# Rearranging the first microseconds of a fused S5 + SwiGLU kernel: fewer warm-up matmuls, a split first tile, and another order of loads

## The chip, the cores and the metric

The kernel runs on one core of a Trainium2 chip. The metric is the device time of one execution in microseconds (us). Before the change it is 183.48 us, the median of three runs (183.38, 183.48 and 184.09).

A core has a matrix engine (TensorE, in the profile PE, with its weight loads as PEld), a vector engine (VectorE, DVE), a scalar engine (ScalarE, ACT), GpSimd (POOL) and a queue engine that issues most DMAs (SyncE, SP). Each engine executes its own list of instructions in order and waits on semaphores for the others.

## The reference

The input x has 2048 rows of 512 values in bf16. Each row is normalised, and the normalised rows go through two branches whose results are added to x:

```python
xn = layernorm(x)                                   # rows of 512, eps 1e-5
# branch A: a diagonal complex state space model with 512 states
Lam_bar = exp(dt * Lam);  B_bar = ((Lam_bar - 1) / Lam)[:, None] * Bmat
h_t = Lam_bar * h_{t-1} + B_bar @ xn_t              # for t in 0..2047
yA  = 2 * real(h @ Cmat.T) + xn * Dskip
# branch B: a gated feed-forward layer of width 1376
yB  = (silu(xn @ w_gate) * (xn @ w_up)) @ w_down
return x + yA + yB
```

## The kernel before, in words

The 2048 rows are cut into 16 tiles of 128 rows and 4 chunks of 4 tiles. The matrix engine needs the normalised rows transposed (features on the partitions); the buffer for that is `xnT`, two chunks deep. For each chunk the matrix engine computes the gate and the up product (11 slices of w_gate and w_up of up to 128 columns, four matmuls of 512 columns each, line 684), the input product of the state space model (line 750), the down product (line 838, with the Dskip term at line 841 for the first two chunks) and the output product of the state space model (line 854). The vector engine does the normalisation, the rotations and the scans; the scalar engine evicts the products from PSUM.

The program is a graph of tasks. `_schedule` lists them for each engine: the lists of the matrix engine and of SP keep the order in which the tasks were added, and those of the other engines come from a list scheduler that uses estimated durations. `_plan` turns dependences into semaphore waits.

The head of the kernel, which the change touches, is the time until the first full-width matmul of the up product. It goes like this:

- SP issues the loads in this order (lines 405 to 416): x tile 0, x tile 1, x tiles 2-3 as one load of 256 KB, the first three gate slices (`ld_wgA`, 384 KB), the next three (`ld_wg0`, 384 KB), the first six up slices (`ld_wu0`, 768 KB), then the other gate and up slices and x tiles 4-7.
- The matrix engine starts with `pe_warm`: ten matmuls of 512 columns on a zeroed tile, whose results nobody reads (line 451). Then come the transposes of the parameter rows (`params_t`, line 460).
- For each of the tiles 0 to 3, `ln_tile` adds bn_stats (line 473), bn_aggr (line 476) and the variance plus eps (`ve`, line 478) on the vector engine, the power -1/2 (`rstd`, line 480) on GpSimd and the normalisation itself (`xn`, line 483) on the vector engine. In the head, the bn_stats of a tile waits for the `ve` of the tile ahead and for the `xn` of two tiles ahead, by real dependences.
- `ffn_gate_quarters` runs six gate slices of the first chunk tile by tile ("quarters" of 128 columns), so that they can start before all four tiles are there. `xt_tile_fine` transposes one tile with four matrix-engine transposes (line 523) and evicts it with one scalar-engine copy of 128x512 (line 529). The order on the matrix engine is: transposes of tiles 0 and 1; 24 gate matmuls of tile 0 (line 712); transposes of tile 2; 24 gate matmuls of tile 1; transposes of tile 3; 24 of tile 2; 24 of tile 3. The up product (line 684, from `ffn_up`) follows.
- Between these, GpSimd and the vector engine compute the parameters (`dt`, line 586; lines 588 and 591), and the scalar engine makes the first tables (`tm`, line 635). The copy of tile 3 stands behind two of these in the scalar engine's list.

Of the kernel before, what the change touches and what calls it, by code (L numbers as in the profile page):

```python
# [10 lines left out]
ALU = alu_op_type.AluOpType  # L11
# [10 lines left out]
    warm=10,  # L22
# [8 lines left out]
class _Task:  # L31
    __slots__ = ("eng", "fn", "deps", "name", "est", "idx", "dma", "sem", "lvl",
                 "waits", "nsig", "vc", "out", "lat", "bl", "start", "fin", "nbytes", "prio", "ninst")
# [5 lines left out]
class _Graph:  # L39
# [5 lines left out]
    def add(self, eng, fn, reads=(), writes=(), name="", est=100.0, dma=False, after=(), out=False, nbytes=0, prio=0.0, ninst=1):  # L45
# [21 lines left out]
        t.deps = deps  # L67
        t.sem = None
# [12 lines left out]
def _schedule(tasks, engines, slack=200.0):  # L81
    succ = defaultdict(list)
    for t in tasks:
        for d in t.deps:
            succ[d].append(t)
# [18 lines left out]
    nun = {t: len(t.deps) for t in tasks}  # L104
# [135 lines left out]
def bass_parallel_sum__ssm_conv_s5__swiglu_ffn__prompt_kernel(  # L240
# [28 lines left out]
    EPS = 1e-5  # L269
# [3 lines left out]
    with es:  # L273
# [135 lines left out]
        dma("ld_x1", x_sb[:, 1:2, :], x_v[:, 1:2, :], [("x", 1)], TILEB)  # L409
        dma("ld_x2", x_sb[:, 2:4, :], x_v[:, 2:4, :], [("x", 2), ("x", 3)], 2 * TILEB)  # L410
        FQ = 3 * 128
        dma("ld_wgA", wg[:, :, 0:FQ], wg_v[:, :, 0:FQ], [("wg", "a")], 512 * FQ * 2)
        dma("ld_wg0", wg[:, :, FQ:FH0], wg_v[:, :, FQ:FH0], [("wg", 0)], 512 * (FH0 - FQ) * 2)
# [55 lines left out]
        ln_prev = [None]  # L469
        ln_xn = {}  # L470

        def ln_tile(a, norm_act):
            g.add("dve", lambda e, a=a: e.bn_stats(out=st[:, a, :], in_=x_sb[:, a, :]),  # L473
                  reads=[("x", a)], writes=[("st", a)], name="bnst%d" % a, est=640,
                  after=(((ln_prev[0],) if (ln_prev[0] is not None and a < 4) else ()) + ((ln_xn[a - 2],) if (a < 4 and (a - 2) in ln_xn) else ())))
            g.add("dve", lambda e, a=a: e.bn_aggr(out=mv[:, a, :], in_=st[:, a, :]),
                  reads=[("st", a)], writes=[("mv", a)], name="bnag%d" % a, est=90)
            ln_prev[0] = g.add("dve", lambda e, a=a: e.tensor_scalar(out=ve[:, a:a + 1], in0=mv[:, a, 1:2], scalar1=EPS, scalar2=None, op0=ALU.add),  # L478
                                reads=[("mv", a)], writes=[("ve", a)], name="ve%d" % a, est=70)
            g.add("pool", lambda e, a=a: e.tensor_tensor(out=rstd[:, a:a + 1], in0=ve[:, a:a + 1], in1=mhalf[:, a:a + 1], op=ALU.pow),  # L480
                  reads=[("ve", a), ("mhalf",)], writes=[("rstd", a)], name="rstd%d" % a, est=400)
# [4 lines left out]
            else:  # L486
# [3 lines left out]
                      reads=[("x", a), ("rstd", a), ("nmr", a)], writes=[("xn", a % NXN)], name="xn%d" % a, est=710)  # L490

# [4 lines left out]
        def xt_chunk(c):  # L496
            a0 = 4 * c
            for pair in range(2):
# [12 lines left out]
                def evac(e, aa=aa, slot=slot):  # L511
# [3 lines left out]
                      writes=[("xnT", c % 2, aa % 4), ("xnT", c % 2, aa % 4 + 1)], name="xTev%d" % aa, est=930)  # L515

        def xt_tile_fine(c, a):
            if True:
                slot = next_tr()

                def tr4(e, a=a, slot=slot):
                    for kt in range(KT):
                        inst = e.transpose(out=ptr[:, slot, kt * 128:(kt + 1) * 128],  # L523
                                           in_=xn_sb[:, a % NXN, kt * 128:(kt + 1) * 128], identity=ident[:])
                    return inst
                g.add("pe", tr4, reads=[("xn", a % NXN), ("ident",)], writes=BK(slot), name="xT%d" % a, est=4 * 64, ninst=4)

                def evac(e, a=a, slot=slot):
                    return e.activation(out=xnT[:, c % 2, a % 4, :, :],  # L529
                                        in_=ptr[:, slot, 0:512].rearrange("p (k t) -> p k t", k=KT), func=AF.Identity)  # L530
                g.add("act", evac, reads=BK(slot), writes=[("xnT", c % 2, a % 4)], name="xTev%d" % a, est=500)

        def xt_chunk_dma(c):
            s0 = (4 * c) % NXN
            dma("xTd%d" % c, xnT[:, c % 2].rearrange("p j k t -> p (j k) t"), xn_sb[:, s0:s0 + 4, :],
                [("xnT", c % 2, j) for j in range(4)], 4 * TILEB, reads=[("xn", s0 + j) for j in range(4)], xpose=True)
# [135 lines left out]
        def wres(nm, i):  # L672
            if nm == "wg" and i < 3:
                return ("wg", "a")
            return (nm, 0 if i < 6 else 1)

        def ffn_mm(c, i, which):
# [9 lines left out]
            g.add("pe", mm, reads=[wres("wg" if which == "g" else "wu", i)] + [("xnT", c % 2, j) for j in range(4)],  # L687
# [12 lines left out]
        def ffn_gate_quarters(c, tiles):  # L700
            xt_tile_fine(c, 4 * c)
            banks = {i: next_bank() for i in tiles}
            for q in range(4):
                for ii, i in enumerate(tiles):
                    if q < 3 and ii == 0:
                        xt_tile_fine(c, 4 * c + q + 1)
# [3 lines left out]
                    def mm(e, bk=bk, i=i, fs=fs, c=c, q=q):  # L710
                        for kt in range(KT):
# [3 lines left out]
                    g.add("pe", mm, reads=[wres("wg", i), ("xnT", c % 2, q)], writes=BK(bk), name="mm_gq%d_%d_%d" % (c, i, q), est=4 * 62, ninst=4)  # L715
# [29 lines left out]
        def ssm_b_unit(c, pt):  # L745
            br, bi = next_bank(), next_bank()
            for ri, bk in ((0, br), (1, bi)):
# [5 lines left out]
                g.add("pe", mm, reads=[("BT", ri, kt) for kt in range(KT)] + [("xnT", c % 2, j) for j in range(4)],  # L753
# [66 lines left out]
        def dc_chunk(c, mid=None, split_last=False):  # L820
# [10 lines left out]
            for (lt, c0, nc_), bk in zip(items, banks):  # L831
# [11 lines left out]
                g.add("pe", mmA, reads=[("hT", hb, i) for i in range(FT)] + [("wd", 0), ("wd", 1)] + ([("xnT", c % 2, lt)] + [("diagD", kt) for kt in range(KT)] if dg else []),  # L843
# [130 lines left out]
```

## Time and profile before

| what | us |
|---|---|
| median of three runs | 183.48 |
| the profiled execution: span from first to last instruction | 181.8 |
| around the span, against the median | 1.7 |
| PE busy | 177.7 (98% of the span) |
| DVE busy | 165.0 (91%) |
| ACT busy | 91.4 (50%) |
| POOL busy | 13.4 (7%) |

The profiled execution has no time of its own beside its span; what lies around the span is taken as the difference to the median, 183.48 - 181.8 = 1.7 us, and counted as constant.

Times inside the profile are given from the start of the span. In the timeline a row has the start, the duration, the engine and the line, the operation, the tiles written and read, and how many instructions were merged; in brackets stands the idle time ahead of it and what ended it. A matrix-engine instruction is shown with its whole latency, so rows overlap: the step from one matmul to the next is shorter than a row's duration. The names out of the matrix engine are `pb` (PSUM banks); `SPq` and `ACTq` are rows in which a queue issues DMAs.

### The profile page before, as it was taken

The numbers are of one execution on the slowest core, as the hardware profiler recorded it, in microseconds if no ns is written. First come the engines' busy times: TensorE is split into PE (matmuls) and PEld (weight loads), VectorE is DVE, ScalarE is ACT, GpSimd is POOL, SyncE is SP. The second block draws the span as 40 slices with busy tenths as digits, with TensorE's granted clock in tenths as the row PEclk, the third lists the DMA queues.
The fourth block names the chain that finished last, engine by engine and source line by source line (L and its number), as shares of the span: only waits on it lengthen the run. The fifth ranks groups of instructions, "written<-read, shape, count | busy, mean of one in ns | idle before, by whom it ended". The sixth has DMA issues, their size and how long they took to land.

```text
span 181.8 us, 2579 instructions
## 1 busy us (share of the span) xinstructions
PE 177.7 (98%) x937; PEld 86.8 (48%) x937; DVE 165.0 (91%) x359; ACT 91.4 (50%) x162; POOL 13.4 (7%) x30
## 2 busy tenths in 40 slices
PE   6999999999999999999999999999999999999994
PEld 2694444444444454444444455444444444444643
DVE  3899878999999998999999999999999999999733
ACT  3299989996899108057666380026677620000000
POOL 5530500000000013000000220000000000000000
DMA  5992666669100000730000000620000000000102
GB/s 146 325 375 61 141 130 108 145 182 346 49 0 4 0 0 0 128 108 0 0 0 0 0 4 0 115 94 22 0 4 2 2 0 0 0 32 29 58 29 87
DMA packets 23388, 12.39 MB, mean 68 GB/s; under 512 B 15088, under 2 KB 23376, under 8 KB 23376
## 3 DMA queue, kind: packets, MB, share of 16 engines
q1 hardware_dynamic: 23344, 12.23, 25.3%
q8 instruction: 7, 0.11, 0.3%
q14 instruction: 5, 0.04, 0.1%
q10 hardware_dynamic: 32, 0.00, 0.0%
HBM read 6.46 MB, written 2.10 MB: 47 GB/s over the span
## 4 chain that ended last, share of the span: by engine, by line
PE 97%; ACT 0%; POOL 0%; DVE 0%; issue 0%; DVEq 0%; POOLq 0%
PE pb L684 39%; PE pb L838 21%; PE pb L854 15%; PE pb L750 15%; PE pb L712 3%; PE pb L451 2%; PE pb L841 1%; PE pb L523 1%; ACT xnT L529 0%; POOL zt L442 0%; DVE osb L865 0%; PE pb L460 0%; POOL mhalf L432 0%; DVEq L234 0%; POOLq L959 0%
## 5 line engine op out<-in xcount | busy, mean ns | idle before, releaser
L684 PE MATMUL pb<-xnT,wu 128*128 128x512 bf16 (+1 forms) x176 | 43.7, 379 | 0.0
L838 PE MATMUL pb<-wd,hT 128*128 128x512 bf16 (+3 forms) x187 | 39.7, 367 | 0.0
L789 DVE TENSOR_TENSOR_SCAN vq<-sm,car,vq 128x512 bf16<-128x512 f32 x32 | 39.5, 1271 | 0.1
L684 PE MATMUL pb<-xnT,wg 128*128 128x512 bf16 (+1 forms) x152 | 38.4, 379 | 0.0
L734 ACT ACTIVATE uf<-pb 128x512 bf16<-128x512 f32 (+1 forms) x44 | 25.4, 603 | 6.8 <-PE pb L684 6.6
L854 PE MATMUL pb<-W,hss 128*128 128x512 bf16 (+1 forms) x136 | 28.3, 366 | 0.0
L750 PE MATMUL pb<-xnT,BT 128*128 128x512 bf16 x128 | 28.1, 379 | 0.0
L684 PEld LDWEIGHTS pb<-xnT,wu 128*128 128x128 bf16 (+1 forms) x176 | 17.6, 100 | 20.1
L838 PEld LDWEIGHTS pb<-wd,hT 128*128 128x128 bf16 (+1 forms) x187 | 18.0, 98 | 18.5
L697 ACT ACTIVATE sg<-pb 128x512 bf16<-128x512 f32 (+1 forms) x38 | 22.5, 597 | 7.5 <-PE pb L684 7.4
L684 PEld LDWEIGHTS pb<-xnT,wg 128*128 128x128 bf16 (+1 forms) x152 | 15.3, 100 | 17.6
L757 ACT ACTIVATE u_sb<-pb 128x512 bf16<-128x512 f32 x16 | 9.6, 600 | 20.5 <-PE pb L750 20.3
L854 PEld LDWEIGHTS pb<-W,hss 128*128 128x128 bf16 x136 | 13.2, 98 | 13.9
L750 PEld LDWEIGHTS pb<-xnT,BT 128*128 128x128 bf16 x128 | 12.5, 98 | 15.1
L736 DVE TENSOR_TENSOR hT<-sg,uf 128x512 bf16<-128x512 bf16 (+1 forms) x44 | 18.1, 416 | 1.2 <-ACT uf L734 0.7
L480 POOL TENSOR_TENSOR rstd<-ve,mhalf 128x1 f32<-128x1 f32 x16 | 9.4, 604 | 90.4 <-DVE ve L478 90.4
L473 DVE BATCH_NORM_STATS2 st<-x_sb 128x6 f32<-128x512 bf16 x16 | 10.4, 685 | 2.9 <-DMA x_sb<-in_A_x_dram 2.8
L780 DVE TENSOR_TENSOR scrA<-u_sb,cosT 128x1024 bf16<-128x1024 bf16 x16 | 10.9, 682 | 0.7 <-ACT u_sb L759 0.7
L489 ACT ACTIVATE xn_sb<-x_sb,nmr,rstd 128x512 bf16<-128x512 bf16 x8 | 5.9, 803 | 10.2 <-POOL rstd L480 8.8
L799 DVE TENSOR_TENSOR scrA<-vq,sin 128x1024 bf16<-128x1024 bf16 x16 | 11.0, 684 | 0.0
L783 DVE TENSOR_TENSOR scrA<-u_sb,sin 128x1024 bf16<-128x1024 bf16 x16 | 10.9, 684 | 0.0
L795 DVE TENSOR_TENSOR scrA<-vq,cosT 128x1024 bf16<-128x1024 bf16 x16 | 10.9, 684 | 0.0
(71 smaller groups left out, 135.8 us busy)
## 6 DMA issues: line engine op xcount, KB each, us to landing
out_dram<-osb SPq DMA_DIRECT2D x15, 128.0 KB, 1.7
x_sb<-in_A_x_dram SPq DMA_DIRECT2D x3, 512.0 KB, 7.6
wd<-in_B_w_down_dram SPq DMA_DIRECT2D x1, 1280.0 KB, 7.0
wg<-in_B_w_gate_dram SPq DMA_DIRECT2D x2, 384.0 KB, 4.6
wu<-in_B_w_up_dram SPq DMA_DIRECT2D x1, 768.0 KB, 7.4
wg<-in_B_w_gate_dram SPq DMA_DIRECT2D x1, 608.0 KB, 8.5
wu<-in_B_w_up_dram SPq DMA_DIRECT2D x1, 608.0 KB, 9.6
x_sb<-in_A_x_dram SPq DMA_DIRECT2D x2, 128.0 KB, 2.2
```

Source lines behind the costliest of these rows:

```text
L684: inst = e.matmul(pbank[0:fs, bk, :].rearrange("p (j t) -> p j t", j=4), lhsT=w[:, kt, i * 128:i * 128 + fs], rhs=xnT[:, c % 2, :, kt, :], ...
L697: g.add("act", lambda e, sl=sl, bk=bk, fs=fs: e.activation(out=sg[0:fs, sl, :], in_=pbank[0:fs, bk, :], func=AF.Silu), reads=BK(bk), write ...
L734: g.add("act", lambda e, ul=ul, bk=bk, fs=fs: e.activation(out=uf[0:fs, ul, :], in_=pbank[0:fs, bk, :], func=AF.Identity), reads=BK(bk), w ...
L736: g.add("dve", lambda e, sl=sl, ul=ul, fs=fs, i=i, hb=hb: e.tensor_tensor(out=hT[0:fs, hb, i, :], in0=sg[0:fs, sl, :], in1=uf[0:fs, ul, :] ...
L750: inst = e.matmul(pbank[:, bk, :].rearrange("p (j t) -> p j t", j=4), lhsT=BT[:, ri, kt, pt * 128:(pt + 1) * 128], rhs=xnT[:, c % 2, :, kt ...
L780: g.add("dve", lambda e, sl=sl, U=U, Cb=Cb: e.tensor_tensor(out=pr2[:, sl, 0], in0=U, in1=Cb, op=ALU.mult), reads=ru + rdt, writes=[("pr", ...
L783: g.add("dve", lambda e, sl=sl, Usw=Usw, S2=S2: e.tensor_tensor(out=pr2[:, sl, 1], in0=Usw, in1=S2, op=ALU.mult), reads=ru + rdt, writes=[ ...
L789: g.add("dve", lambda e, sl=sl, ri=ri, pt=pt, rr=rr, c=c: e.tensor_tensor_scan(out=vq[:, sl, 1, ri, :], data0=rr[:, pt:pt + 1].to_broadcas ...
L795: g.add("dve", lambda e, sl=sl, Q=Q, Cb=Cb: e.tensor_tensor(out=po2[:, sl, 0], in0=Q, in1=Cb, op=ALU.mult), reads=rq + rdt, writes=[("po", ...
L799: g.add("dve", lambda e, sl=sl, Qsw=Qsw, S2sw=S2sw: e.tensor_tensor(out=po2[:, sl, 1], in0=Qsw, in1=S2sw, op=ALU.mult), reads=rq + rdt, wr ...
L838: inst = e.matmul(pbank[:, bk, 0:nc_], lhsT=hT[0:fs, hb, i, lt * 128:(lt + 1) * 128], rhs=wd[0:fs, i, c0:c0 + nc_], start=(i == 0), stop=F ...
L854: inst = e.matmul(pbank[:, bk, 0:nc_], lhsT=hss[:, hb, pt, ri, lt * 128:(lt + 1) * 128], rhs=W12[:, ri, pt, c0:c0 + nc_], start=False, sto ...
```

## The change

Five edits, all in the head:

1. `warm` goes from 10 to 8: two of the zero matmuls are taken out.
2. The six gate slices come as one load of 768 KB (rows of 1536 bytes instead of twice 768), and this load stands ahead of x tiles 2-3 in SP's list.
3. Tile 0 is transposed and evicted in two halves (two transposes and a copy of 128x256 each), in two PSUM banks. The 24 gate matmuls of tile 0 are cut likewise: 12 that contract over the first half, then the transposes of tile 1, then the 12 that contract over the second half.
4. The transposes of tiles 2 and 3 go into the middle of a tile's gate matmuls: after two of the six slices, the four others follow behind the transposes.
5. The order of the normalisation in the vector engine's list is set by order-only edges (`order=`, no semaphore): bn_stats of tile a behind `ve` of tile a-1, bn_aggr of tile a behind `xn` of tile a-1. The planner's estimate for `rstd` goes from 400 to 600 ns, with a priority for the head.

The order that the planner makes of this: on the matrix engine 8 warm-ups, the parameter transposes, the 4 transposes of tile 0, 12 gate matmuls, the 4 of tile 1, 20 gate matmuls, the 4 of tile 2, 24, the 4 of tile 3, 40, and then the up product as before. On the vector engine the head becomes: bn_stats 0, bn_aggr 0, `ve` 0, bn_stats 1, `xn` 0, bn_aggr 1, `ve` 1, `xn` 1, the copy of the parameters (line 463), bn_stats 2, bn_aggr 2, `ve` 2, bn_stats 3, `xn` 2, bn_aggr 3, `ve` 3, four diagD (line 466), the two parameter operations (before: lines 588 and 591), `xn` 3. GpSimd's and SP's lists are otherwise as before; the scalar engine has one copy more, and the copy of tile 3 again stands behind two `tm`.

```diff
-    warm=10,
+    warm=8,
...
         dma("ld_x0", x_sb[:, 0:1, :], x_v[:, 0:1, :], [("x", 0)], TILEB)
         dma("ld_x1", x_sb[:, 1:2, :], x_v[:, 1:2, :], [("x", 1)], TILEB)
+        dma("ld_wg0", wg[:, :, 0:FH0], wg_v[:, :, 0:FH0], [("wg", 0)], 512 * FH0 * 2)
         dma("ld_x2", x_sb[:, 2:4, :], x_v[:, 2:4, :], [("x", 2), ("x", 3)], 2 * TILEB)
-        FQ = 3 * 128
-        dma("ld_wgA", wg[:, :, 0:FQ], wg_v[:, :, 0:FQ], [("wg", "a")], 512 * FQ * 2)
-        dma("ld_wg0", wg[:, :, FQ:FH0], wg_v[:, :, FQ:FH0], [("wg", 0)], 512 * (FH0 - FQ) * 2)
         dma("ld_wu0", wu[:, :, 0:FH0], wu_v[:, :, 0:FH0], [("wu", 0)], 512 * FH0 * 2)
...
         def ln_tile(a, norm_act):
-            g.add("dve", lambda e, a=a: e.bn_stats(out=st[:, a, :], in_=x_sb[:, a, :]),
-                  reads=[("x", a)], writes=[("st", a)], name="bnst%d" % a, est=640,
-                  after=(((ln_prev[0],) if (ln_prev[0] is not None and a < 4) else ()) + ((ln_xn[a - 2],) if (a < 4 and (a - 2) in ln_xn) else ())))
-            g.add("dve", lambda e, a=a: e.bn_aggr(out=mv[:, a, :], in_=st[:, a, :]),
-                  reads=[("st", a)], writes=[("mv", a)], name="bnag%d" % a, est=90)
...
+            head = a < 4
+            ln_bn[a] = g.add("dve", lambda e, a=a: e.bn_stats(out=st[:, a, :], in_=x_sb[:, a, :]),
+                             reads=[("x", a)], writes=[("st", a)], name="bnst%d" % a, est=640,
+                             order=((ln_ve.get(a - 1),) if head else ()))
+            ln_ag[a] = g.add("dve", lambda e, a=a: e.bn_aggr(out=mv[:, a, :], in_=st[:, a, :]),
+                             reads=[("st", a)], writes=[("mv", a)], name="bnag%d" % a, est=90,
+                             order=((ln_xn.get(a - 1),) if head else ()))
...
-                  reads=[("ve", a), ("mhalf",)], writes=[("rstd", a)], name="rstd%d" % a, est=400)
+                  reads=[("ve", a), ("mhalf",)], writes=[("rstd", a)], name="rstd%d" % a, est=600, prio=(3000.0 if head else 0.0))
...
+        def xt_tile_fine(c, a, parts=1):
+            n = KT // parts
+            for h in range(parts):
                 slot = next_tr()
+                k0 = h * n
+
+                def tr(e, a=a, slot=slot, k0=k0):
+                    for kt in range(k0, k0 + n):
+                        inst = e.transpose(out=ptr[:, slot, (kt - k0) * 128:(kt - k0 + 1) * 128],
                                            in_=xn_sb[:, a % NXN, kt * 128:(kt + 1) * 128], identity=ident[:])
                     return inst
+                g.add("pe", tr, reads=[("xn", a % NXN), ("ident",)], writes=BK(slot), name="xT%d_%d" % (a, h), est=n * 64, ninst=n)
+
+                def evac(e, a=a, slot=slot, k0=k0):
+                    return e.activation(out=xnT[:, c % 2, a % 4, k0:k0 + n, :],
+                                        in_=ptr[:, slot, 0:n * 128].rearrange("p (k t) -> p k t", k=n), func=AF.Identity)
+                g.add("act", evac, reads=BK(slot), writes=(XN(c, a % 4) if parts == 1 else [XN(c, a % 4)[h]]), name="xTev%d_%d" % (a, h), est=130 + 90 * n)
...
         def ffn_gate_quarters(c, tiles):
-            xt_tile_fine(c, 4 * c)
+            xt_tile_fine(c, 4 * c, parts=2)
             banks = {i: next_bank() for i in tiles}
...
+            for q in range(4):
+                if q == 0:
+                    quarter(q, tiles, 0, 1)
+                    xt_tile_fine(c, 4 * c + 1)
+                    quarter(q, tiles, 1, 2)
+                else:
+                    quarter(q, tiles[:2], 0, 2)
+                    if q < 3:
+                        xt_tile_fine(c, 4 * c + q + 1)
+                    quarter(q, tiles[2:], 0, 2)
```

`quarter(q, ts, h0, h1)` adds the gate matmuls of tile q for the slices in `ts` over the halves h0 to h1 of the contraction; `XN(c, j)` names the two halves of tile j in `xnT`. Every other reader of `xnT` now waits for both halves.

## The prediction

> **What bounds the kernel now.** I read the chain that ended last first, in order of time (start, length, engine, tile and line):
>
> ```profile
> 1.42 4.45 PE pb L451 x10
> ...
> 6.63 0.61 ACT xnT L529
> ...
> 7.29 1.59 PE pb L712 x24
> ...
> 10.66 2.68 PE pb L712 x48
> 13.34 13.81 PE pb L684 x64
> 27.15 13.81 PE pb L750 x64
> ```
>
> From line 684 on the chain is the matrix engine without a gap, 13.81 / 64 = 0.216 us a matmul; and no other engine stands in the chain between 7.3 and 179 us. So this change is worth exactly what it does to the start of the first up matmul, provided that nothing later comes to wait. In the timeline that start is 13.18 us (the chain gives 13.34, the end of the piece ahead).
>
> Next the timeline of the head, DVE and ACT rows:
>
> ```profile
> 2.84 0.69 DVE L473 BATCH_NORM_STATS2 st<-x_sb 128x6 f32<-128x512 bf16 x1 [2.84 <-DMA x_sb<-in_A_x_dram]
> 3.97 0.69 DVE L473 BATCH_NORM_STATS2 st<-x_sb 128x6 f32<-128x512 bf16 x1
> 5.28 0.69 DVE L473 BATCH_NORM_STATS2 st<-x_sb 128x6 f32<-128x512 bf16 x1
> 8.00 0.41 DVE L483 TENSOR_SCALAR xn_sb<-x_sb,mv,rstd 128x512 bf16<-128x512 bf16 x1 [0.41 <-POOL rstd L480]
> 8.53 0.15 DVE L478 TENSOR_SCALAR ve<-mv 128x1 f32<-128x1 f32 x1
> 9.41 0.41 DVE L483 TENSOR_SCALAR xn_sb<-x_sb,mv,rstd 128x512 bf16<-128x512 bf16 x1
> 9.93 1.34 ACT L635 ACTIVATE scrC<-iot,sm 128x512 f32<-128x512 f32 x2 [0.20 <-DVE sm L588]
> 11.18 0.57 ACT L529 ACTIVATE xnT<-pb 128x512 bf16<-128x512 bf16 x1
> ```
>
> Tile 2's bn_stats starts at 5.28 because the vector engine is busy, not because x tiles 2-3 are late. Tile 3's copy (11.18) comes in time for the matmuls of tile 3. What starts the gate matmuls at 7.29 is tile 0's copy.
>
> Then the loads. Single issues (start) and their time to landing, asked of one issue each, give the landing times: x tile 0 0.79 + 2.0 = 2.8, x tile 1 1.25 + 2.3 = 3.5, tiles 2-3 1.71 + 3.0 = 4.7, first gate slices 2.18 + 3.9 = 6.1, next ones 2.69 + 5.3 = 8.0, six up slices 3.25 + 7.4 = 10.6. The windows view shows the rate (its last column):
>
> ```profile
> 3.00:4.00 1.00, 1.00 (x4) 0.35 (x3) 0.90 (x4) 0.00 (x0) 0.00 (x0) 1.00 0.91 260
> 4.00:5.00 1.00, 1.00 (x4) 0.40 (x3) 0.96 (x3) 0.00 (x0) 0.56 (x1) 1.00 0.98 282
> 5.00:6.00 1.00, 1.00 (x8) 0.20 (x6) 0.94 (x3) 0.00 (x0) 0.55 (x1) 1.00 0.89 257
> 6.00:7.00 1.00, 0.96 (x11) 0.67 (x8) 0.84 (x5) 0.37 (x1) 0.66 (x1) 1.00 1.06 333
> ```
>
> The DMA engines are full (the column before, 0.89 to 1.06) from 2 us on, and the loads land in the order of issue. A load that is moved back pays for the bytes put ahead of it.
>
> **The change, part by part.**
>
> Two warm-ups less: the chain has 4.45 / 10 = 0.445 us each, so the last one ends near 5.0 instead of 5.86. The parameter transposes follow at about 5.0 and take 0.2. They need the last parameter row; nothing shows when it landed except that the transposes ran at 5.79, so the gain here is 0 to 0.85 us, and I take all but a little of it. It is not on the final path (below).
>
> Tile 0: `xn` 0 now stands ahead of bn_aggr 1 and starts near 4.7 instead of 4.80, ends 5.1. Its transposes run near 5.15 instead of 5.99. A copy of 128x256 has no row; it lies between the 0.21 of a 128x4 ACT row and the 0.60 of 128x512, in proportion to the elements 0.40. The first half is copied by about 6.0, the second, which overlaps it, by 6.4.
>
> The joined gate load: the six up slices have the same shape, and took 10.6 - 8.0 = 2.6 us behind the load ahead of them. Behind x tile 1 that gives 3.5 + 2.6 = 6.1; at the 257 to 282 GB/s of that stretch 786 KB would take 2.8 to 3.1, so 6.3 to 6.6. I take 6.3. The gate matmuls can start at 6.35 instead of 7.29, a gain of 0.9 if nothing came after. Bounds 6.1 to 6.8.
>
> x tiles 2-3: 768 KB now go ahead of them where nothing did. Best row: the joined load by its like (2.6) and their own 4.7 - 3.5 = 1.1 after it, so 3.5 + 2.6 + 1.1 = 7.2. Worst: the same 1280 KB, in the present order and in narrower rows, were complete at 8.0. I take 7.4, nearer to the first because the rows are as wide as there. Call this L; the bounds are 7.0 and 8.0.
>
> Now tile 2 is late, and the vector engine stands at its bn_stats with everything of the head behind it. Its steps from rows: bn_stats at L + 0.03; bn_stats 3 comes 3.97 - 2.84 = 1.13 later and takes 0.69; `xn` 2 follows, start L + 1.89, end L + 2.30 (0.41). GpSimd's `rstd` (0.56) fits between, since `dt` ends before 8. The transposes of tile 2 start at L + 2.35. From there the matrix engine has left, in its new order, 8 transposes and 64 gate matmuls, at (10.27 - 8.93) / 24 = 0.056 us each: 72 x 0.056 = 4.03. So the up product starts at L + 6.38 if it never waits again.
>
> It waits a little. `ve` 3 starts at L + 2.41 (bn_aggr and `ve` follow `xn` 2 by 8.53 - 8.00 = 0.53), four diagD, the two parameter operations now ahead of `xn` 3 (0.15 each at most) and `xn` 3 follow: 9.41 - 8.53 = 0.88, plus 0.17, so `xn` 3 ends at L + 3.87, just as the matrix engine gets there. But the copy of tile 3 stands behind the two `tm` of 1.34 (they start when the first parameter operation is done, L + 3.36, and 11.18 - 9.93 = 1.25 later comes the copy): it starts at L + 4.6, ends L + 5.17, and the last 24 matmuls (1.34) end at L + 6.57. With L = 7.4 the up product starts at 13.97 instead of 13.18: 0.8 us later. Wherever L is above 6.6, the change loses one for one with it.
>
> Between tile 1's first matmuls and tile 2's transposes the matrix engine would stand still for about one us; that, not the copy of tile 0, is the new wait. All matmuls and transposes of real data are kept. The vector engine's order costs nothing by itself, since the DMA wait hides it.
>
> Behind the head: the later loads keep their order and total bytes, the next one landing at about 10, where 13.2 is needed. DVE ends the head L + 3.87 - 0.17 - 9.82 = 1.3 late, half a us more than PE. It has 10 - 7.42 = 2.6 us of idle time between 20 and 30, and waits for ACT's u_sb, which follows PE, at 29.95, so this is absorbed. The nearest deadline later is the DMA transpose of chunk 2 (issued at 71.70 when ACT has normalised, 4.5 to landing, 76.2; PE wants it at 77.11): 0.9 of slack, moving along with both.
>
> Sum: -0.9 (earlier start of the gates) and +1.7 (waits for tiles 2 and 3) = +0.8. The profiled execution's 181.8 and the 1.7 around it make the median, 183.48; prediction 184.3.
>
> **The rivals.**
>
> The pair is early (ends on the other side). If the DMA engines brought x tiles 2-3 before 6.6, the change would do what it says. After x tile 1 (3.5) they must bring 1.05 MB. At the 333 GB/s of the fourth row this takes 3.15 us: L = 6.65 and no change, 183.5. At the 395 GB/s that the windows view shows for 9 to 10 us, L = 6.2 and 183.0. For a gain above 0.5% L would have to be 5.7, 477 GB/s, which no stretch has. Against it: from 3 to 6 us the traffic ran at 257 to 282. [...]
>
> The clock comes late. The warm-ups take 0.445 us each where the up matmuls take 0.216 (half rate), and the transposes at 6.64 still step by about 0.1 us, those at 8.71 by 0.056: full speed came between 6.9 and 7.3. With two warm-ups less and a pause after them it could come later. Ahead of tile 2's transposes stand 36 gate matmuls and transposes: cold they take 3.85 us from 6.35 and end at 10.2, 0.45 past L + 2.35 = 9.75. If the clock is up by then, 184.7; each further us of half rate costs 0.5. For: a longer pause. Against: a like amount of work between 3.5 and 7. [...]
>
> DVE's delay is not absorbed and the transpose of chunk 2 comes late: above 0.9 us of extra delay each us costs one. Up to 185.1. The idle time at 20 to 30 speaks against it.
>
> **How the numbers follow.** Late tile 2: 0.62, 184.3, its own range 183.9 to 184.9 (L from 7.0 to 8.0). Early pair: 0.14, 183.0 to 183.5. Late clock: 0.18, about 184.7. DVE: 0.04; the rest 0.02. I draw the range 183.2 to 185.1. The bound of 0.5%, about what a measurement can tell, is 0.92 us: slower than that needs L above 7.5, some 0.4 of the first case and most of the next, together 0.45. Faster than that: 0.03. Within: 0.52.
>
> **What would show it.** In the profile after: gate matmuls from about 6.3; bn_stats of tile 2 waiting for the DMA at 7.2 to 8.0; a gap of the matrix engine ahead of tile 2's transposes of about one us and a smaller one ahead of the last 24 matmuls, released by ACT; the first up matmul near 14.0; from there the same distances as now. Wrong would be: bn_stats of tile 2 before 6.6, or half-rate steps in the gate matmuls, or a gap of PE after 14.

## The result, and the profile after

The changed kernel takes 185.71 us, the median of five runs (185.54 to 186.44), beside 183.85 us for the kernel before in five runs: ratio 1.012, interval 1.010 to 1.014. The prediction was 184.3 with a range up to 185.1, counted from the 183.48 of the first three runs. From there the loss is 2.2 us where 0.8 was forecast, 1.4 us more, and the range did not hold it. (All ratios leave out runs that lie more than 1.5% above the fastest of their kernel; these are 187.04 us in one experiment and 187.82 in another.)

The profiled execution took 186.44 us (span 184.7, so 1.7 around it, as before); it is the slowest of the five. The timeline of its matrix engine, from the end of the zero matmuls on (start, duration, engine and line, operation, tiles, count, and in brackets the idle time ahead and what ended it):

```profile
6.58 0.24 PE L460 MATMUL pb<-ident,prow 4*128 4x4 bf16 x4 [1.57 <-DMA prow<-in_A_Dskip_dram]
6.75 0.61 PE L535 MATMUL pb<-ident,xn_sb 128*128 128x128 bf16 x4
7.62 1.46 PE L721 MATMUL pb<-xnT,wg 128*128 128x128 bf16 x12 [0.26 <-ACT xnT L541]
...
9.30 2.34 PE L721 MATMUL pb<-xnT,wg 128*128 128x128 bf16 x20
11.44 0.63 PE L535 MATMUL pb<-ident,xn_sb 128*128 128x128 bf16 x4
11.86 1.87 PE L721 MATMUL pb<-xnT,wg 128*128 128x128 bf16 x24
13.57 0.39 PE L535 MATMUL pb<-ident,xn_sb 128*128 128x128 bf16 x4
13.79 2.40 PE L721 MATMUL pb<-xnT,wg 128*128 128x128 bf16 x40
16.02 0.81 PE L694 MATMUL pb<-xnT,wu 128*128 128x512 bf16 x3
```

In the kernel before, tile 2's transposes and the first up matmul were here:

```profile
8.71 0.39 PE L523 MATMUL pb<-ident,xn_sb 128*128 128x128 bf16 x4
...
13.18 5.34 PE L684 MATMUL pb<-xnT,wu 128*128 128x512 bf16 x24
```

Three things are to be seen. The first up matmul starts at 16.02 instead of 13.18, 2.84 later, and the span is 2.9 longer, so the whole loss lies ahead of it. The engine stood 1.57 us at the parameter transposes, waiting for a row of 1 KB. And the gate matmuls are at half rate for a long time: 12 in 1.46 and 20 in 2.34, about 0.11 each, until the 24 that start at 11.86; only the last 40 have the full rate from the start (13.79 to 16.02, 0.056 each).

The chain that ended last, in order of time (start, length, what), has the same row in it, and shows that behind the head nothing changed:

```profile
2.07 4.37 DMA prow<-in_A_Dskip_dram
...
13.95 2.23 PE pb L721 x40
16.19 13.81 PE pb L694 x64
30.00 13.81 PE pb L772 x64
```

The Dskip row, issued at 2.07 on ACT's queue, took 4.37 us to land (at 6.44); in the trace of the kernel before, the same issue took 2.35 and landed at 4.42, and no wait showed it. (Landings that no view names are from the trace's records of the semaphores.) Up product and input product are 13.81 each, as before.

The vector engine's rows show the step that the prediction was about:

```profile
7.75 0.69 DVE L476 BATCH_NORM_STATS2 st<-x_sb 128x6 f32<-128x512 bf16 x1 [0.73 <-DMA x_sb<-in_A_x_dram]
...
9.51 0.41 DVE L487 TENSOR_SCALAR xn_sb<-x_sb,mv,rstd 128x512 bf16<-128x512 bf16 x1
```

Tile 2 is late: x tiles 2-3 landed at 7.73. But its normalised rows are there at 9.9, and the matrix engine comes for them only at 11.44, because it is at half rate. So in this execution no wait for the late tile lies on the path: the late row and the half rate hide it. The runs with the clock on time, below, show it again.

### The profile page after: what moved, and what is told of

Same layout as the page of the kernel before. It is cut to its first block, busy times and chain, and to the rows that moved or that the text cites. A ratio compares the mean times of both kernels' runs of the same rounds, so it can differ in the third digit from the quotient of the medians.

```text
span 184.7 us, 2573 instructions
## 1 busy us (share of the span) xinstructions
PE 178.9 (97%) x935; PEld 88.7 (48%) x935; DVE 166.4 (90%) x359; ACT 92.4 (50%) x163; POOL 13.6 (7%) x30
## 3 DMA queue, kind: packets, MB, share of 16 engines
HBM read 6.46 MB, written 2.10 MB: 46 GB/s over the span
## 4 chain that ended last, share of the span: by engine, by line
PE 95%; DMA 2%; ACTq 0%; ACT 0%; DVE 0%; issue 0%; DVEq 0%
PE pb L694 38%; PE pb L860 21%; PE pb L876 15%; PE pb L772 15%; PE pb L721 4%; DMA prow<-in_A_Dskip_dram 2%; PE pb L863 1%; PE pb L535 1%; ACTq L393 0%; DVE osb L887 0%; ACT xnT L541 0%; ACT L443 0%; PE pb L460 0%; DVEq L236 0%
## 5 line engine op out<-in xcount | busy, mean ns | idle before, releaser
L756 ACT ACTIVATE uf<-pb 128x512 bf16<-128x512 f32 (+1 forms) x44 | 26.0, 601 | 16.2 <-DVE hT L758 8.9
L779 ACT ACTIVATE u_sb<-pb 128x512 bf16<-128x512 f32 x16 | 9.5, 593 | 21.5 <-PE pb L772 21.5
L476 DVE BATCH_NORM_STATS2 st<-x_sb 128x6 f32<-128x512 bf16 x16 | 10.2, 680 | 3.6 <-DMA x_sb<-in_A_x_dram 3.6
L781 ACT ACTIVATE u_sb<-pb 128x512 bf16<-128x512 f32 x16 | 9.6, 597 | 2.8 <-PE pb L772 2.1
```

The source lines that it names most:

```text
L756: g.add("act", lambda e, ul=ul, bk=bk, fs=fs: e.activation(out=uf[0:fs, ul, :], in_=pbank[0:fs, bk, :], func=AF.Identity), reads=BK(bk), w ...
```

## The experiments

All kernels here compute the whole reference. The first four quoted texts weigh three theories: C, the clock comes late; W, the wait for the Dskip row alone decides; L, the late x tiles are the whole loss. From the fifth on the leading theory, P, holds that two separate things cost time: the order of the loads (the joined load ahead makes the Dskip row and tile 2 late), and the clock (with fewer warm-ups and a pause, full speed comes late). Its rivals hold that one of the two does it all, or that the new interleaving does.

One number ties the runs together. In every profiled execution the time from the first up matmul to the end of its own measured time is the same: 186.44 - 16.02 = 170.42 for the changed kernel, and 170.31 to 170.44 in eleven of the twelve experiments. So the column "first up" below is the time, but for one kernel. The clock column is from the clock records of the trace: when full speed was granted. (The spans that the texts of e6 and e10 expect for it, 4.1 to 7.5 and 5 to 8.3, follow from no run; their profiled executions had it from 6.06 and 5.79.)

| kernel | full speed from | first up | profiled | median |
|---|---|---|---|---|
| before | no record | 13.18 | span 181.8 | 183.48 |
| after | 12.62 | 16.02 | 186.44 | 185.71 |
| e1, after with 10 warm-ups | 5.77 | 14.05 | 184.47 | 184.62 |
| e6, after with 13 | 6.06 | 14.15 | 184.56 | 184.56 |
| e4, after, Dskip row apart | 5.82 | 13.89 | 184.25 | 184.48 |
| e3, after, x tiles 2-3 first | 6.02 | 13.95 | 184.39 | 184.96 |
| e2, before with 8 (lists moved) | 10.37 | 14.98 | 185.36 | 185.68 |
| e5, before with 8 (same lists) | 4.76, lost 8.17 to 11.58 | 15.05 | 185.36 | 183.73 |
| e8, before with the new loads | 6.49 | 14.62 | 184.94 | 184.89 |
| e9, after with the old loads | no record | 13.59 | 183.90 | 183.92 |
| e7, head rearranged | 7.38 | 14.19 | 185.96 | 185.93 |
| e10, e11, e12, early gates | 5.79, 5.10, 5.43 | 13.19, 13.50, 12.78 | 183.53, 183.93, 183.19 | 183.54, 183.94, 183.27 |

(The kernel before took 183.45 to 183.49 in the runs beside the experiments.)

### The warm-ups (e1 and e6)

```diff
-    warm=8,
+    warm=10,
```

> The changed kernel with ten warm-up matmuls again, all else as changed. In its profile the matrix engine stood still from 4.80 to 6.58 us, waiting for the Dskip parameter row (landed 6.4), and the gate matmuls then ran at half rate (0.107 us) until 12.6; the first up matmul came at 16.0 instead of 13.2. Theory C (the clock comes late because too little ran on the matrix engine before about 7 us): with two more warm-ups the pause is 0.9 us instead of 1.8, full speed comes near 7.3, and the first up matmul is set by x tiles 2-3 (landed 7.7): about 14.3, time 185.0. Rival W (the wait for the Dskip row alone decides, warm-ups count for nothing): still a pause, still half rate past 10 us, up matmul at 15.3 to 16.0, time 185.7. Rival L (the late x tiles are the whole loss, clock without effect on the end): time as changed, 185.7.

Measured: 184.62 us, ratio 1.0067 (1.0042 to 1.0093). Two zero matmuls more take 1.1 us off the changed kernel's median; one of the four runs is still at 185.49.

With 13 of them, and the planner's estimate kept so that every other list stays the same:

```diff
-    warm=8,
+    warm=13,
...
-            g.add("pe", mm, ..., name="pe_warm", est=n * 430, ninst=n)
+            g.add("pe", mm, ..., name="pe_warm", est=8 * 430, ninst=n)
```

> The changed kernel with thirteen warm-up matmuls, all other lists as in it. [...] Theory P: full speed near 4.1 to 7.5 in every execution, times within 0.4 us of each other, and the up matmul set by x tiles 2-3 at their landing (7.4 to 7.7) + 6.5 = 13.9 to 14.2 or by the gates that start at 7.9 (7.9 + 6.05 = 13.95): 184.3 to 184.6 where the kernel before has 183.48. Rival (warm-ups do not matter, the spread comes from elsewhere): times as in the changed kernel, 185.5 to 186.4.

Measured: 184.56 us, ratio 1.0061 (1.0049 to 1.0073). Its timeline:

```profile
6.60 0.25 PE L460 MATMUL pb<-ident,prow 4*128 4x4 bf16 x4
...
7.54 0.84 PE L721 MATMUL pb<-xnT,wg 128*128 128x128 bf16 x12 [0.36 <-ACT xnT L541]
...
9.95 0.40 PE L535 MATMUL pb<-ident,xn_sb 128*128 128x128 bf16 x4
...
14.15 2.54 PE L694 MATMUL pb<-xnT,wu 128*128 128x512 bf16 x11
```

The parameter transposes and the gates start when they did in the changed kernel (6.58 and 7.62 there), so this run removes nothing but the half rate: 12 gate matmuls take 0.84 instead of 1.46. That alone is worth 1.88 us between the two profiled executions and 1.15 between the medians. It also shows what is left with the clock on time: 1.1 us above the kernel before. The zero matmuls themselves hide completely behind the wait for the Dskip row.

### The warm-ups in the kernel before (e2 and e5)

```diff
-    warm=10,
+    warm=8,
```

> The kernel before with eight warm-up matmuls, all else as before. [...] Rival W: the Dskip row lands at 4.4 as before, so nothing waits, the clock comes as before, up matmul near 13.0, time 183.6. Rival L: loads as before, time 183.6 to 183.9.

Measured: 185.68 us in ten runs spread from 184.08 to 187.04, ratio 1.0111 (1.0075 to 1.0146). This run doesn't isolate what it was meant to: the warm-ups' estimate is part of the plan, and with 8 the planner put the parameters ahead of tile 1's `rstd`, so that tile 1 was transposed at 7.67. It was repeated with the plan held:

```diff
-    warm=10,
+    warm=8,
...
-            g.add("pe", mm, ..., name="pe_warm", est=n * 430, ninst=n)
+            g.add("pe", mm, ..., name="pe_warm", est=4300, ninst=n)
```

> The kernel before with eight warm-up matmuls, the planner's estimate for them left as it was, so that no other engine's list changes (in the first try the planner also moved the parameter copy ahead of tile 1, which came 1 us later for it). [...] Theory C as first put (the number of warm-ups decides, always late): all at 185 or above. Rival L (loads alone): all at 183.4 to 183.8.

Measured: 183.73 us, ratio 1.0031 (1.0009 to 1.0053), and the eleven runs fall into groups: six from 183.41 to 183.73, four from 184.52 to 184.75, and the profiled one at 185.36. The windows view of that one (stretch, busy time and count of PE, PEld, DVE, ACT and POOL, then the granted clock, the DMA share and GB/s):

```profile
4.80:8.10 3.30, 1.79 (x25) 1.28 (x24) 2.75 (x11) 1.19 (x2) 2.18 (x3) 1.00 1.03 334
8.20:11.50 3.30, 3.10 (x30) 3.10 (x31) 2.30 (x15) 1.18 (x3) 1.62 (x2) 0.50 1.07 390
11.60:14.00 2.40, 2.40 (x46) 2.40 (x45) 2.33 (x5) 1.98 (x4) 0.00 (x0) 1.00 0.86 285
```

```profile
6.90 0.83 PE L712 MATMUL pb<-xnT,wg 128*128 128x128 bf16 x12
8.40 1.46 PE L712 MATMUL pb<-xnT,wg 128*128 128x128 bf16 x12 [0.67 <-DMA wg<-in_B_w_gate_dram]
```

Full speed was granted at 4.76, taken back for 3.41 us after a stretch in which the engine mostly waited (by the steps of its rows it worked for about 1.3 of the 3.4 us), and granted again: the same 12 matmuls take 0.83 before 8 us and 1.46 after. So in this kernel the two warm-ups are not worth a fixed time but a chance: six of eleven runs lose nothing, the others one to two us. What the four runs near 184.6 lost was not profiled; a late clock there too is not shown. (In a stretch ahead of the first clock record the column says 1.00 at half rate too: it does so in every us from 7 to 12 of the changed kernel, whose gates step by about 0.107 there.)

### The Dskip row out of the way (e4)

```diff
         def params_t():
-            ... for k in range(4): transpose prow[k]      # one task, four rows
+            params_rows(0, 3, "a")
+        def params_d():
+            params_rows(3, 4, "d")                        # the Dskip row, and diagD behind it
...
         (end of the gate quarters)
+            params_d()
```

> The changed kernel in which the Dskip row is transposed by itself, behind the gate matmuls, with its diagonal tiles behind it; so the first parameter transposes wait for three rows (landed by 3.6) and run at about 4.95, tile 0's transposes at 5.2, gates at 6.5 when the joined load lands. Theory C: a pause from 5.6 to 6.5 remains and warm-ups are eight; the clock comes late or in time depending on how much of the time before 7 us was busy; if late, half rate until 10 or beyond and the up matmul at 14.5 to 15.2 (185.2 to 185.9). Rival W: clock on time, up matmul at 14.3 by x tiles 2-3 (185.0). Rival L: 14.3, 185.0 as well, since the tiles are as late as in the changed kernel.

Measured: 184.48 us, ratio 1.0051 (1.0035 to 1.0068), with 8 warm-ups.

```profile
4.94 0.23 PE L460 MATMUL pb<-ident,prow 4*128 4x4 bf16 x3
...
6.57 0.83 PE L727 MATMUL pb<-xnT,wg 128*128 128x128 bf16 x12 [0.77 <-DMA wg<-in_B_w_gate_dram]
...
9.66 0.40 PE L541 MATMUL pb<-ident,xn_sb 128*128 128x128 bf16 x4 [0.51 <-DVE xn_sb L493]
...
13.89 2.98 PE L700 MATMUL pb<-xnT,wu 128*128 128x512 bf16 x13
```

This is the head that the prediction described: parameter transposes at 4.94, gates behind the joined load, a wait for tile 2, and the up product at 13.89 where 13.97 was forecast. With the row out of the way the clock comes at 5.82 without a warm-up more: tile 0's transposes now follow at 5.20, and the engine is busy for 0.78 of the us from 5 to 6, where in the changed kernel it was 0.01. So the row's wait and the missing warm-ups act together, and repairing either is enough in nearly every run: of the thirteen runs of this kernel and of the two with 10 and 13 warm-ups, twelve lie between 184.25 and 184.82.

### The loads (e3, e8 and e9)

x tiles 2-3 ahead of the joined load, in the changed kernel:

```diff
+        dma("ld_x2", x_sb[:, 2:4, :], ...)
         dma("ld_wg0", wg[:, :, 0:FH0], ...)
-        dma("ld_x2", x_sb[:, 2:4, :], ...)
```

> The changed kernel with x tiles 2-3 loaded ahead of the joined gate load, all else as changed. Tiles 2-3 land near 4.7 and the joined load near 7.3, where the gate matmuls can start. Theory C: still eight warm-ups and now a pause from 5.6 to 7.3, so half rate until 10.5 to 12.5: up matmul between 14.9 and 15.9, time 185.5 to 186.5. Rival L: the late tiles are gone, up matmul at 7.35 + 6.05 = 13.4, time 184.1. Rival W: the parameter row lands by about 4.5 again, so the clock is on time: 184.1.

Measured: 184.96 us in six runs (184.38 to 187.82), ratio 1.0078 (1.005 to 1.0105).

```profile
7.36 0.83 PE L721 MATMUL pb<-xnT,wg 128*128 128x128 bf16 x12 [1.56 <-DMA wg<-in_B_w_gate_dram]
...
13.95 2.75 PE L694 MATMUL pb<-xnT,wu 128*128 128x512 bf16 x12
```

Tile 2 is early (its load landed at 5.04), but the joined load lands at 7.22 and the gates, which need all of it for their first pass over the six slices, start at 7.36. One wait goes and another comes, so the early tiles gain little: 13.95, where the joined load ahead gave 13.89 to 14.15 with the clock on time. (The planner also puts tile 2's bn_stats ahead of tile 1's `xn` here.) In the profiled execution the clock was on time (6.02) with eight warm-ups, against the quoted expectation: tile 0's transposes, at 5.18, follow the zero matmuls closely. Three of the six runs are above 185.4. One of these, 185.54, has a mean granted clock of 0.991, the mean of e5's profiled run, where full speed was taken back for 3.41 us (last section); the other two have 1.0, and what they lost is not shown. Without the 187.82 the median is 184.43.

The new loads in the kernel before, with its 10 warm-ups:

```diff
-        dma("ld_x2", ...);  dma("ld_wgA", wg[:, :, 0:FQ], ...);  dma("ld_wg0", wg[:, :, FQ:FH0], ...)
+        dma("ld_wg0", wg[:, :, 0:FH0], ...);  dma("ld_x2", ...)
```

> The kernel before with the new loads alone: the six gate slices as one load of 768 KB ahead of x tiles 2-3; ten warm-up matmuls, no split, the old interleaving (the planner puts tile 1's normalisation and the parameters' copy ahead of bn_stats of tile 2). Theory P (loads and clock both count, the clock separately from the loads): the Dskip row lands at 5.9 to 6.5 instead of 4.4, x tiles 2-3 at L = 7.4 to 7.7; tile 2's transposes start at L + 2.35, and behind them stand 8 transposes and 72 gate matmuls at 0.056 = 4.5 us, so the up product starts at about L + 6.85 = 14.3, 1.1 later: 184.6 (184.3 to 185.0), with the clock on time in most executions. [...]

Measured: 184.89 us, ratio 1.0083 (1.0059 to 1.0108).

```profile
6.67 0.23 PE L458 MATMUL pb<-ident,prow 4*128 4x4 bf16 x4 [0.81 <-POOL rstd L478]
...
9.94 0.40 PE L521 MATMUL pb<-ident,xn_sb 128*128 128x128 bf16 x4 [0.43 <-DVE xn_sb L481]
...
14.62 1.24 PE L680 MATMUL pb<-xnT,wu 128*128 128x512 bf16 x5
```

The loads alone cost 1.4 us with the clock on time (full speed from 6.49). The Dskip row lands at 6.46 here too, which is what the transposes at 6.67 wait for (the releaser named, a `rstd`, had ended long before); and tile 2's transposes come 1.2 later than the 8.71 of the kernel before. One of the four runs, 185.73, has a mean granted clock of 0.991, with ten warm-ups.

The rest of the change with the old loads and 10 warm-ups:

```diff
-    warm=8,
+    warm=10,
...
-        dma("ld_wg0", wg[:, :, 0:FH0], ...);  dma("ld_x2", ...)
+        dma("ld_x2", ...);  dma("ld_wgA", wg[:, :, 0:FQ], ...);  dma("ld_wg0", wg[:, :, FQ:FH0], ...)
```

> The changed kernel with the loads of before (x tiles 2-3 ahead, gate slices as 384 + 384 KB) and ten warm-ups: the split of tile 0, the new interleaving and the order on the vector engine alone. Theory P: the Dskip row lands at 4.4 and tile 2 is early again, so nothing of the 2.2 us remains; the gate matmuls start near 7.0, but the first half of tile 0 now asks for slices 3 to 5 (landing at 8.0) before tile 1's transposes, so 102 gate matmuls and transposes at 0.056 stand behind 8.0: first up matmul 13.6 to 13.8, 183.9 (183.6 to 184.3). The rival (the new interleaving is what costs): above 184.4.

Measured: 183.92 us in ten runs, ratio 1.0034 (1.0011 to 1.0056).

```profile
7.69 0.51 PE L725 MATMUL pb<-xnT,wg 128*128 128x128 bf16 x6 [0.32 <-DMA wg<-in_B_w_gate_dram]
...
13.59 2.10 PE L698 MATMUL pb<-xnT,wu 128*128 128x512 bf16 x9
```

The Dskip row lands at 4.72 again. The split and the new interleaving are no gain by themselves but cost 0.4: tile 0's first half already asks for slices 3 to 5, which land at 7.64, with only 6 gate matmuls done. One of the ten runs, 185.79, has the clock of 0.991 again.

### Versions meant to be faster (e7, e10, e11 and e12)

First the whole head again on the changed kernel: the Dskip row apart, one zero matmul behind tile 0's transposes, the loads as x0, x1, slices 0-2, x2, slices 3-5, x3, and the tables behind tile 3's copy.

```diff
+        dma("ld_wgA", wg[:, :, 0:FQ], ...);  dma("ld_x2", x_sb[:, 2:3, :], ...)
+        dma("ld_wg0", wg[:, :, FQ:FH0], ...);  dma("ld_x3", x_sb[:, 3:4, :], ...)
...
-  name="tm%d" % pt, ..., prio=_CFG['prio_tab'])
+  name="tm%d" % pt, ..., prio=_CFG['prio_tab'], order=(last_ev[0],))    # last_ev: tile 3's copy
```

> Another head, from what the runs showed: eight warm-ups, three parameter rows ahead and the Dskip row behind the gate matmuls of tile 0, one more zero matmul between tile 0's transposes and the gates; loads in the order x 0, x 1, three gate slices, x 2, three gate slices, x 3; gate matmuls of tile 0 on the first three slices from about 6.1, the other three when they land (7.4); the tables of the scalar engine behind tile 3's copy. Theory P: no pause of the matrix engine longer than 0.5 us before 7, so the clock is on time in every execution; the up matmul is at 7.45 + 84 x 0.056 + 8 x 0.056 = 12.6 to 12.8 instead of 13.2: 182.9 to 183.2, below the kernel before. If the clock is late in some executions, those lie at 184 to 186. Rival: a wait not counted (x 3, its copy) puts it at 13.2 or later, 183.5.

Measured: 185.93 us, ratio 1.0131 (1.0117 to 1.0146), though its first up matmul is at 14.19. This is the one kernel whose rest is longer, 171.77 instead of 170.4. The longest wait of its matrix engine behind the start (us in total, times, longest):

```profile
PE pb L795 <- DMA xnT<-xn_sb: 1.2, 1, 1.2
```

The DMA transpose of chunk 2 was issued at 74.90 instead of 71.70, 3.2 later, where the matrix engine was only 1.0 later; of these 2.2 us, 0.9 were slack and 1.2 became a wait. The vector engine had waited for the held-back tables: it was busy for 17.7 of the 20 us from 30 to 50, 19.9 before. That the tables alone made it late was not tested apart. So the prediction's fourth case, with its 0.9 us of slack, is real, and the changed kernel did not reach it: there the transpose landed 2.8 later (79.05 beside 76.22), as much as the matrix engine came later.

The next three keep the loads of before. Eight warm-ups, tile 0 in halves, one zero matmul behind its transposes; slices 0 to 2 of tiles 0 and 1 ahead of slices 3 to 5; the copies of tiles 2 and 3 each ahead of one `tm`.

```diff
+            pe_fill(banks[tiles[5]], 1)
+            quarter(0, tiles[:3], 0, 1);  xt_tile_fine(c, 4 * c + 1);  quarter(0, tiles[:3], 1, 2)
+            quarter(1, tiles[:3], 0, 2);  quarter(0, tiles[3:], 0, 2)
+            last_ev[1] = xt_tile_fine(c, 4 * c + 2)
+            quarter(1, tiles[3:], 0, 2);  quarter(2, tiles[:3], 0, 2)
+            last_ev[0] = xt_tile_fine(c, 4 * c + 3)
+            quarter(2, tiles[3:], 0, 2);  quarter(3, tiles, 0, 2)
```

> [...] Theory P: parameter transposes at 5.0, tile 0's transposes at 5.2, gates from 6.2 to 6.5 instead of 7.3, full speed between 5 and 8.3, the last 24 gate matmuls from 11.2 to 11.5, first up matmul 12.5 to 13.0: 182.8 to 183.3. The rival of the run with the rearranged head (holding the tables back makes the vector engine late for the transposed load of chunk 2): the up product early, but a wait of about 1 us at the input product of chunk 2, 183.8 to 184.5.

Measured: 183.54 us, ratio 1.001 (0.9989 to 1.0032): no difference. The gates start at 6.11, 1.2 us earlier, and give it back:

```profile
7.66 1.51 PE L735 MATMUL pb<-xnT,wg 128*128 128x128 bf16 x24 [0.35 <-ACT xnT L552]
```

The engine waits for tile 1's copy, and twice more for 0.18 for those of tiles 2 and 3. In the next one tile 1 comes in halves as well, and the transposes of tiles 2 and 3 stand further ahead of the first matmul that reads them.

```diff
-            xt_tile_fine(c, 4 * c + 1)
+            xt_tile_fine(c, 4 * c + 1, parts=2)
...
-            quarter(0, tiles[3:], 0, 2);  last_ev[1] = xt_tile_fine(c, 4 * c + 2)
+            last_ev[1] = xt_tile_fine(c, 4 * c + 2);  quarter(0, tiles[3:], 0, 2)
...
-            quarter(2, tiles[:3], 0, 2);  last_ev[0] = xt_tile_fine(c, 4 * c + 3);  quarter(2, tiles[3:], 0, 2)
+            last_ev[0] = xt_tile_fine(c, 4 * c + 3);  quarter(2, tiles, 0, 2)
```

> The version with early gates and the loads of before, with two of its waits taken out: tile 1 is transposed and evicted in two halves as well, and the transposes of tiles 2 and 3 stand 24 gate matmuls or more ahead of the first matmul that reads them. Theory P: gates of tile 1 at about 7.4 instead of 7.66, the two waits of 0.18 gone, slices 3 to 5 landing at 7.7 just in time; 92 matmuls and transposes at 0.056 = 5.15 behind 7.4: first up matmul 12.6 to 12.7 instead of 13.19, 182.9 to 183.1. The rival (the vector engine's tables come later and the transposed load of chunk 2 with them, or another wait takes the place): 183.4 or more, with a gap of the matrix engine behind the head in the profile.

Measured: 183.94 us, ratio 1.0021 (1.0011 to 1.003). The median is 0.4 above that of the version ahead of it, though the two intervals overlap.

```profile
9.26 1.50 PE L735 MATMUL pb<-xnT,wg 128*128 128x128 bf16 x24 [0.78 <-ACT xnT L552]
```

The first matmul of slice 3 waits for tile 2's copy, though it doesn't read tile 2: PSUM banks go round over transposes and products alike, and these transposes had a bank of slices 3 to 5 that nothing had written yet. With that step back in its place, and tile 3's transposes kept early:

```diff
-            last_ev[1] = xt_tile_fine(c, 4 * c + 2);  quarter(0, tiles[3:], 0, 2)
+            quarter(0, tiles[3:], 0, 2);  last_ev[1] = xt_tile_fine(c, 4 * c + 2)
```

> The same version with one step moved: tile 2's transposes stand behind the gate matmuls of tile 0's slices 3 to 5 instead of ahead of them, since in the run before they took the PSUM bank of one of these slices, whose first matmul then waited 0.78 us for tile 2's copy. Theory P: slices 3 to 5 start at about 8.1, no wait behind it but small ones, first up matmul 12.5 to 12.8: 182.8 to 183.1, that is faster than the kernel before by 0.2 to 0.4%. The rival (the distance of up matmul to the end is no longer the same, since the vector engine becomes late): an early up product and 183.4 or more.

Measured: 183.27 us in eleven runs, ratio 0.9993 (0.9984 to 1.0002).

```profile
6.05 0.51 PE L735 MATMUL pb<-xnT,wg 128*128 128x128 bf16 x6
...
12.78 2.98 PE L708 MATMUL pb<-xnT,wu 128*128 128x512 bf16 x13
```

The waits view names no wait behind the start any more, and the first up matmul comes 0.4 earlier than in the kernel before. In time that is 0.1%, and the interval includes no change: of the 1.2 us by which the gates start earlier, a third arrives. The rest goes to tile 1's four transposes, which now stand behind the first gates (0.2), to two short stops at tile 1 (0.35), and to 0.3 by which the first up matmul waits for the end of the scalar engine's first `sg` eviction (12.72).

## Why the prediction was wrong, point by point

**What bounds the kernel.** Right. The loss is the delay of the first up matmul (2.84 of 2.9), and the rest keeps its length.

**The loads.** Right in size. The joined load landed at 6.45 (forecast 6.3), x tiles 2-3 at 7.73 (7.4, bounds 7.0 to 8.0). With the clock on time, the forecast rule "first up at L + 6.57" gives 14.27 for the run with 13 warm-ups (L = 7.70; measured 14.15), 14.18 for 10 (L = 7.61; 14.05), and 13.98 with the row apart (L = 7.41; 13.89). The first case, 184.3, is what these runs show: 184.5 to 184.6.

**The step that failed first: "two warm-ups less".** It said that the parameter transposes follow at about 5.0, that the last parameter row's landing isn't shown, and that "the gain here is 0 to 0.85 us". The bound left out a loss. The joined load was priced for x tiles 2-3, which stand behind it in SP's list, but not for the 1 KB rows on the other queue that were in flight beside it. The Dskip row landed 2.0 us later (6.44), and the transposes at 6.58 instead of 5.0; tile 0's transposes, and with them the gates, stood behind them in the engine's list: 7.62 instead of 6.35. By itself this would have been covered by the wait for tile 2: the run with 13 warm-ups has the same start and ends up where the first case puts it.

**The step that failed in the end: the price of the late clock.** The rival was named, with 0.18 and 0.4 us more than the first case. Its reasoning was that the 36 cold gate matmuls and transposes end at 10.2, just past the arrival of tile 2, so that the wait covers them. Two things were wrong in it. The start was 7.62, not 6.35, so nothing was left of the cover (the engine reached tile 2 at 11.44, 1.5 after its data). And full speed was taken to be up when those 36 end, at 10.2; in the profiled execution the half rate lasted to 12.62. The 64 gate matmuls and transposes from 7.62 to 13.57 took 5.95 us, 2.3 more than at the 0.057 each of the kernel before (104 from 7.29 to 13.18). With the gates' later start of 0.33 and tile 1's four transposes, which now stand behind the first gates (0.2), that makes the 2.84. The medians put the clock's share at 1.1 to 1.2 us (185.71 beside 184.56). The rival's own rule, 0.5 for each further us of half rate, gives 184.7 + 1.2 = 185.9 with half rate to 12.62 instead of 10.2, an estimate near the median of 185.71 (the profiled execution took 186.44): the price per us was about right, and the length was wrong. The prediction's own sign of being wrong, half-rate steps in the gate matmuls, is there. "Against: a like amount of work between 3.5 and 7" did not hold: the matrix engine was busy for 3.46 of these 3.50 us in the kernel before and for 1.93 in the changed one, since the removed 0.85 us and the new pause both lie there.

**The early pair.** Rightly held unlikely: L was above 7.4 in every run with the new order. **DVE and chunk 2.** Right that the change doesn't reach it; the rearranged head, where 2.2 us of extra delay became 1.2 us of waiting, agrees with the slack of 0.9.

## What to carry to other kernels

A load that is moved ahead or made larger can delay what is in flight beside it, here by 2 us even a 1 KB row on another queue: ask of each row that an engine needs early when it landed, and where the profile doesn't show that, bound it from both sides. In these runs the warm-up matmuls were worth something where they filled a pause (185.71 us with it open, 184.56 with 13 of them in it); take them out only where real work follows closely (184.48 with the Dskip row apart), and read several executions, since one of them tells only its own time: the eleven of e5 lie between 183.41 and 185.36. When a wait is to hide another cost, check that the first one still stands when both are moved.

## What the runs showed of the hardware

The clock records say when full speed was granted, and the rows what the matrix engine did ahead of it. In the changed kernel the eight zero matmuls ran from 1.41 to 4.80 by their steps of 0.43, nothing followed until 6.58, and full speed came at 12.62 and stayed to the end of the span. With the same eight, and tile 0's transposes behind them at 5.18 and 5.20, it came at 6.02 (e3) and 5.82 (e4). With ten zero matmuls (to 5.66) it came at 5.77 (e1) and 6.49 (e8), with thirteen at 6.06 (e6). In e2, where the engine stood for 0.65 us ahead of tile 0's transposes and for 1.23 ahead of tile 1's, it came at 10.37. In e7, where tile 0's transposes follow at 5.28, a zero matmul at 5.68 and the gates at 6.15, it came at 7.38, and with much the same rows up to there in e10, e11 and e12 at 5.79, 5.10 and 5.43. In e5 it came at 4.76, with the eighth zero matmul not yet through. What decides the time of a grant is not shown by these runs: how busy the engine was ahead of it, as theory C has it, was not tested apart.

None of the changed kernel's five runs was as fast as the 184.6 of the runs with the clock on time. Two of the five, 185.75 and 185.68, have a mean granted clock of 0.991. So has the profiled run of e5, where full speed was taken back once: half of 3.41 us in 183.6 is 0.009. Nine runs in these tables have this clock, in six kernels, and all nine lie between 185.36 and 185.79. That full speed came early and was taken back for 3.41 us in the other eight as well is an estimate from that mean; these eight were not profiled. The other two of the five that were not profiled (185.71 and 185.54) have 1.0, as the profiled one with its late grant; that they too had a late grant is not shown.

In e5 full speed was taken back after 3.41 us (4.76 to 8.17) in which the engine worked for about 40% by its steps. In e8, e3 and e4 it worked for 55 to 59% of the first 3.41 us after the grant, and full speed stayed.

The small row's 2.35 us on ACT's queue became 4.37 when 768 KB were issued on SP's queue at 1.71, just ahead of it; with the old loads it was back (4.72 at landing). It goes with the size of the load issued there: the row landed at 5.91 to 6.63 in the five profiled runs with 768 KB, at 5.38 with 384 KB (e7), and at 4.42 to 4.80 in the eight with the 256 KB of x tiles 2-3. The parameter row ahead of it, issued at 1.73, was not delayed (3.55 beside 3.50). The mechanism of that sharing was not tested.
